# Gate and up projections with their last 64 contraction rows as two 64-row TensorE tiles, weight loads in single pieces, and a prologue with the layer norm per tile

## The chip, the cores and the metric

One NeuronCore of a Trainium2 chip runs the whole program. The metric is device time in microseconds, from the profiler or the device timer; the median of three timed executions of the kernel before is 284.12 us (283.15 to 285.14). The engines are TensorE (PE for its matmuls, PEld for its weight loads), VectorE (DVE), ScalarE (ACT), GpSimd (POOL) and SyncE (SP, which here issues almost all DMAs, in the order of its own queue).

## The reference

The input x has 2048 rows of 448 columns. Four segments of 512 rows are processed in order; there are 16 heads of 28 columns.

```python
h = _layernorm(x) * (1 + ca) + sa
x = x + ga * _A_ref(h, wq, wk, wv, wo, beta)
h = _layernorm(x) * (1 + cb) + sb
x = x + gb * _B_ref(h, w_gate, w_up, w_down)

# A, per segment s and head:
p = softmax(qs @ ks.T * scale + mask)          # causal inside the segment
a_mem = (phi(qs) @ M) / (phi(qs) @ z + 1e-6)   # memory of the segments before
o = sigmoid(beta) * a_mem + (1 - sigmoid(beta)) * (p @ vs)
M = M + phi(ks).T @ vs ;  z = z + sum(phi(ks))
# B:
out = (sigmoid(h @ w_gate) * (h @ w_up)) @ w_down   # 448 -> 1792 -> 448
```

The six vectors sa, ca, ga, sb, cb, gb come from silu(c) @ w_mod. Everything is bf16 with fp32 accumulation.

## The kernel before, in words

The 448 columns are the contraction of every projection. They are cut into three chunks of 128 rows and one of 64 (LW = 64); the weight tiles have four chunks, and rows 64 to 127 of the fourth are zeros, so each projection runs four matmuls of 128 rows. The 1792 columns of gate and up are cut into 14 chunks of 128 (NFC, the index fc).

Per segment: layer norm (class LN: stats, rstd, norm on DVE and POOL, then a transposition into hT, either by DMA on SP's queue in norm_t or by TensorE in pe_chunk, then a scale and shift called modulate); eight projections for q and k and four for v (proj_jobs); per group of four heads hc three groups of logits matmuls (logits, g = 0, 1, 2), each into the one PSUM buffer lg of four banks, emptied by one ACT exponential (line 389); pv, which multiplies by v and by the memory and normalises on DVE; otr, a DMA transposition of the head group's output; wo_tile with the residual and the statistics of the second norm; gate_up for each fc (four gate matmuls into gps, tanh on ACT into tt, four up matmuls into ups, one DVE operation into fT); down, 14 matmuls per 128 rows, and the store.

All other PSUM tiles (gps, ups, acc, mem, pq, pv, dps and so on) come from one ring of four banks (ps_m, tag "m"): a new tile waits for the readers of the one four allocations before it.

The order of the work is written out: there is no scheduler (manual_schedule). The loop at the end goes over the 4 x 4 head groups and their three logits groups; after each it takes jobs from the queue fill until their estimated cost reaches a rate. Operations that would have to wait are put off with later(ns, ...) and come out when the estimated clock has advanced so far. Each engine then works strictly in this order. The loads of the weights are jobs of the queue as well: w_gate, w_up and w_down (load_ffn, load_wd) as one DMA of 128-row chunks each, plus one for the 64-row rest of the first two, all on SP.

A row of gate_up is

```python
for k in range(NK):
    nc.tensor.matmul(gp[:, 0:L], lhsT=wg_sb[:, k, fs], rhs=h[:, k, :], start=(k == 0), stop=(k == NK - 1))
```

and the logits use four 32-row tiles of the array side by side, each with 28 rows of contraction:

```python
nc.tensor.matmul(lg[:, hs, wid:wid + nq], lhsT=kT[r, hc, kb * P:(kb + 1) * P],
                 rhs=qT[r, hc, kb * P:L], start=True, stop=True, tile_position=(HP * hs, 0))
```

The prologue runs 24 warm-up matmuls, the statistics of the first four tiles, one rstd for all four, four norms, copies of wq and wk out of a staging area into padded tiles (pad_copy, wq on ACT, wk on DVE), the columns sa and ca (mod_cols), 16 TensorE transposes, and the first two projections.

## Time and profile before

| quantity | value |
| --- | --- |
| median of three timed executions | 284.12 us (283.15 to 285.14) |
| the profiled execution, its own time | 282.85 us |
| its span, first to last instruction | 281.1 us |
| PE busy | 250.8 us (89%), 2025 matmul records |
| DVE busy | 187.4 us (67%) |
| ACT busy | 140.8 us (50%) |
| POOL busy | 70.8 us (25%) |
| mean granted clock of TensorE | 0.976 |
| HBM read | 10.67 MB |

A matmul is recorded from its start to the end of its pipeline, so busy time of PE overlaps itself; what a matmul costs in a stream is read from the starts of neighbours. In timeline rows consecutive instructions of one line are merged: start, length, engine, line, operation, count, and in brackets the idle time of the engine before the row with what ended it.

### The profile page before, as it was taken

How to read it: one execution, taken by the hardware profiler on the slowest of the kernel's cores; microseconds unless marked ns; L12 is line 12 of the kernel's file. 1: busy time of each engine (PE TensorE's matmuls, PEld its weight loads, DVE VectorE, ACT ScalarE, POOL GpSimd, SP SyncE). 2: the span in 40 equal slices, each digit the busy share in tenths (PEclk: the TensorE clock that was granted, in tenths of full speed). 3: DMA queues.
4: the chain of work that ended last, by engine and by line, in shares of the span. 5: the costliest groups of instructions: out<-in, count | busy, mean ns of one | idle time of the engine just before them, and what ended most of it. 6: DMA issues, size and time to landing. Idle time of an engine off the chain costs nothing. (4 is left out here: it accounts for less than half of the span.)

```text
span 281.1 us, 5201 instructions
## 1 busy us (share of the span) xinstructions
PE 250.8 (89%) x2025; PEld 123.0 (44%) x2048; DVE 187.4 (67%) x426; ACT 140.8 (50%) x171; POOL 70.8 (25%) x127
## 2 busy tenths in 40 slices
PE   1989897983888999998797999889999999899995
PEld 0434453541453544544353554435545444344452
DVE  7578899910679778999655858976577493433321
ACT  2268798583365788765165667562662310133300
POOL 1109434331234034144312213521220040000000
PEclk9999998896699999999999999999999999999999
DMA  5998046699412001301211001141300012100001
GB/s 152 294 249 255 2 105 197 118 198 230 104 21 56 23 19 21 75 21 37 54 54 36 21 0 21 37 57 34 55 19 4 18 37 70 35 0 0 2 16 49
DMA packets 40848, 19.66 MB, mean 70 GB/s; under 512 B 29560, under 2 KB 39928, under 8 KB 40824
## 3 DMA queue, kind: packets, MB, share of 16 engines
q1 hardware_dynamic: 39608, 18.30, 29.2%
q10 hardware_dynamic: 1216, 1.03, 1.3%
q8 instruction: 16, 0.26, 0.4%
q14 instruction: 8, 0.07, 0.1%
HBM read 10.67 MB, written 1.84 MB: 44 GB/s over the span
## 5 line engine op out<-in xcount | busy, mean ns | idle before, releaser
L389 ACT ACTIVATE pT<-lg 128x2048 bf16<-128x2048 f32 (+1 forms) x48 | 76.5, 1594 | 48.6 <-PE lg L386 48.6
L397 POOL TENSOR_SCALAR_AFFINE_SELECT pT<-pT 128x512 bf16<-128x512 bf16 x64 | 43.9, 700 | 87.8 <-ACT pT L389 87.8
L487 DVE SCALAR_TENSOR_TENSOR fT<-tt,ups 128x512 bf16<-128x512 f32 x56 | 37.8, 683 | 35.9 <-PE ups L484 24.6
L479 PE MATMUL gps<-hT,wg_sb 128*128 128x512 bf16 x213 | 57.9, 380 | 3.5 <-DVE hT L257 2.6
L481 ACT ACTIVATE tt<-gps 128x512 f32<-128x512 f32 x56 | 33.0, 596 | 53.9 <-PE gps L479 49.4
L484 PE MATMUL ups<-hT,wu_sb 128*128 128x512 bf16 x219 | 56.6, 379 | 2.4 <-DVE t L439 1.5
L493 PE MATMUL dps<-wd_sb,fT 128*128 128x448 bf16 x224 | 44.2, 353 | 2.3 <-DVE fT L487 2.3
L484 PEld LDWEIGHTS <-wu_sb 128*128 128x128 bf16 x224 | 21.5, 98 | 30.1 <-DVE t L439 2.5
L479 PEld LDWEIGHTS <-wg_sb 128*128 128x128 bf16 x224 | 20.4, 97 | 28.9 <-issue 7.4
L493 PEld LDWEIGHTS <-fT 128*128 128x128 bf16 x224 | 21.4, 98 | 23.5 <-DVE fT L487 2.5
L497 DVE TENSOR_TENSOR ot<-dps,x_sb 128x448 bf16<-128x448 f32 x16 | 9.9, 622 | 23.3 <-PE dps L493 23.3
L411 PEld LDWEIGHTS <-pT 128*128 128x128 bf16 x640 | 18.4, 96 | 4.9 <-issue 2.0
L323 PE MATMUL pv<-wv_sb,hT 128*128 128x448 bf16 x64 | 14.7, 372 | 6.1 <-DVE kT L316 6.1
L238 DVE BATCH_NORM_STATS2 st<-x_sb 128x6 f32<-128x448 bf16 x32 | 19.7, 617 | 0.6
L311 PE MATMUL pq<-hT,wq_sb 128*128 128x512 bf16 x61 | 17.9, 391 | 2.5 <-DVE hT L257 1.3
L242 POOL TENSOR_SCALAR rs<-mv 128x1 f32<-128x1 f32 (+1 forms) x20 | 5.1, 255 | 59.0 <-DVE mv L239 59.0
L411 PE MATMUL acc<-vt,pT 128*128 128x29 bf16 x640 | 18.5, 175 | 1.4 <-ACT vt L325 1.4
L386 PE MATMUL lg<-qT,kT 28*128 28x512 bf16 (+3 forms) x256 | 17.6, 307 | 0.9 <-DVE kT L316 0.8
L311 PE MATMUL pq<-hT,wk_sb 128*128 128x512 bf16 x60 | 17.0, 392 | 1.1 <-ACT qT L314 0.7
L257 DVE TENSOR_SCALAR hT<-hT,cols 128x512 bf16<-128x512 bf16 x24 | 9.6, 447 | 12.4 <-DMA hT<-xn 12.3
L246 DVE TENSOR_SCALAR xn<-x_sb,mv,rs 128x448 bf16<-128x448 bf16 x32 | 15.3, 494 | 2.4 <-POOL rs L243 2.3
L243 POOL TENSOR_TENSOR rs<-rs,mhalf 128x1 f32<-128x1 f32 (+1 forms) x20 | 13.7, 683 | 1.7
(81 smaller groups left out, 232.6 us busy)
## 6 DMA issues: line engine op xcount, KB each, us to landing
wm<-in_w_mod_dram SPq DMA_DIRECT2D x5, 392.0 KB, 4.2
out_dram<-ot SPq DMA_DIRECT2D x16, 112.0 KB, 1.7
wd_sb<-in_B_w_down_dram SPq DMA_DIRECT2D x1, 1568.0 KB
x_sb<-in_A_x_dram SPq DMA_DIRECT2D x3, 448.0 KB, 5.5
wg_sb<-in_B_w_gate_dram SPq DMA_DIRECT2D x1, 1344.0 KB, 11.3
wu_sb<-in_B_w_up_dram SPq DMA_DIRECT2D x1, 1344.0 KB
wm<-in_w_mod_dram ACTq DMA_DIRECT2D x1, 392.0 KB, 6.1
wo_sb<-in_A_wo_dram SPq DMA_DIRECT2D x4, 98.0 KB
```

The costliest lines, as they stand in the source:

```text
L238: nc.vector.bn_stats(st[:], self.srcs[i])
L246: nc.vector.tensor_scalar(self.xn[:, i, 0:D], self.srcs[i], self.mv[:, i, 0:1], self.rs[:, i:i + 1], op0=ALU.subtract, op1=ALU.mult)
L311: nc.tensor.matmul(pq[:, 0:L], lhsT=head_cols(w_sb, k, hc), rhs=h[:, k, :], start=(k == 0), stop=(k == NK - 1))
L386: nc.tensor.matmul(lg[:, hs, wid:wid + nq], lhsT=kT[r, hc, kb * P:(kb + 1) * P], rhs=qT[r, hc, kb * P:L], start=True, stop=True, tile_posi ...
L389: nc.scalar.activation(pT[:, :, w0:w0 + wid], lg[:, :, 0:wid], AF.Exp, scale=scale)
L397: nc.gpsimd.affine_select(out=blk, in_=blk, compare_op=ALU.is_ge, fill=0.0, base=0, pattern=[[0, 4], [1, P]], channel_multiplier=-1)
L411: nc.tensor.matmul(accv[:, qb, hs, 0:ME], lhsT=pT[:, hs, c0:c0 + P], rhs=vt[:, kb, hc * 4 + hs, 0:ME], start=(kb == 0), stop=(kb == qb))
L479: nc.tensor.matmul(gp[:, 0:L], lhsT=wg_sb[:, k, fs], rhs=h[:, k, :], start=(k == 0), stop=(k == NK - 1))
L481: nc.scalar.activation(tt[:], gp[:, 0:L], AF.Tanh, scale=0.5)
L484: nc.tensor.matmul(up[:, 0:L], lhsT=wu_sb[:, k, fs], rhs=h[:, k, :], start=(k == 0), stop=(k == NK - 1))
L487: nc.vector.scalar_tensor_tensor(ft[:], tt[:], 1.0, up[:, 0:L], op0=ALU.add, op1=ALU.mult)
L493: nc.tensor.matmul(dp[:, 0:D], lhsT=fT_of[(s, fc)][:, t * P:(t + 1) * P], rhs=wd_sb[:, fc, :], start=(fc == 0), stop=(fc == NFC - 1))
```

## The change

In gate_up a job now has two column chunks: six gate matmuls (three 128-row chunks for each), then the two 64-row rests of gate and of up as four matmuls on two 64-row tiles of the array (rows 0 to 63 hold the rest of w_gate, rows 64 to 127 that of w_up, in one tile wgu_sb), then six up matmuls. For this the 64 last columns of the normed x are copied once more beside themselves (LN.norm, key "2"), so that both halves of the fourth chunk of hT hold them, and the scale and shift columns likewise (mod_cols).

The loads of w_gate and w_up become three DMAs of one 128-row chunk and one of 64 rows each, that of w_down four DMAs of up to four fc; spread puts one of them behind every second job. The modulate of the second norm is put off with later instead of standing in the job before gate_up. From segment 2 on the wo tiles alternate with left-over gate_up jobs, and the rate is set anew in each segment (pace, KEEP). In the prologue x is loaded ahead of c, the memset that the warm-up reads comes first, rstd runs for two tiles at a time, the warm-up is 20 and later 2 matmuls, the transposes follow each tile's norm, and a third projection stands ahead of the first logits. The normalisation in pv uses inverted coefficients, which saves one small DVE operation.

```diff
-    NWARM, TAIL_GU = 24, 9
+    NWARM, EARLY, KEEP = (20, 2), 2400.0, (0, 2, 2, 4)
-    wg_sb = wts.tile([P, NK, F], BF16)
-    wu_sb = wts.tile([P, NK, F], BF16)
+    wg_sb = wts.tile([P, 3, F], BF16)
+    wu_sb = wts.tile([P, 3, F], BF16)
+    wgu_sb = wts.tile([P, F], BF16)
...
         def norm(self, i):
             nc.vector.tensor_scalar(self.xn[:, i, 0:D], self.srcs[i], self.mv[:, i, 0:1], self.rs[:, i:i + 1],
                                     op0=ALU.subtract, op1=ALU.mult)
+            if self.key[0] == "2":
+                nc.vector.tensor_copy(self.xn[:, i, D:DP], self.xn[:, i, D - LW:D])
...
         later(1500, lambda: ln.norm_t(t), ("ln2", s))
+        if t == TPS - 1:
+            for kc in range(NK):
+                later(6500 + 400 * kc, lambda kc=kc: ln.modulate(kc, 2), ("ln2", s))
...
+        fcs = (f0, f0 + 1)
+        fs = [slice(fc * P, (fc + 1) * P) for fc in fcs]
+        gp = [m_f32("gps") for _ in fcs]
+        for g, f in zip(gp, fs):
+            for k in range(3):
+                nc.tensor.matmul(g[:, 0:L], lhsT=wg_sb[:, k, f], rhs=h[:, k, :], start=(k == 0), stop=False)
+        up = [m_f32("ups") for _ in fcs]
+        tts = []
+        for g, u, f in zip(gp, up, fs):
+            for dst, r, first in ((g, 0, False), (u, LW, True)):
+                nc.tensor.matmul(dst[:, 0:L], lhsT=wgu_sb[r:r + LW, f], rhs=h[r:r + LW, 3, :], start=first,
+                                 stop=not first, tile_position=(r, 0))
+            tt = work.tile([P, L], F32, tag="tt", bufs=3)
+            nc.scalar.activation(tt[:], g[:, 0:L], AF.Tanh, scale=0.5)
+            tts.append(tt)
+        for fc, u, f, tt in zip(fcs, up, fs, tts):
+            for k in range(3):
+                nc.tensor.matmul(u[:, 0:L], lhsT=wu_sb[:, k, f], rhs=h[:, k, :], start=False, stop=(k == 2))
...
+    fill.extend(spread(j0[3:6] + sp(late_consts) + j0[6:10] + [ln1_start(2)] + j0[10:] + ln1_pe_jobs(1) + m[0][0:1]
+                       + j1[:8], early_loads, 2))
+    fill.extend([ln1_start(3)] + m[1][0:1] + j1[8:] + [(1000, prep_b1)])
+    fill.extend(spread(j2[:4] + m[0][1:] + j2[4:8] + [(2000, prep_b2)], [piece_wd(f, min(f + 4, NFC)) for f in range(0, NFC, 4)], 2))
...
+                    for w in wo_jobs(s - 1):
+                        fill.append(w)
+                        if tail and s > 1:
+                            fill.append(tail.pop(0))
+                    fill.extend(tail)
...
+                    pace[0] = (cost(fill) - KEEP[s] * GU) / (12 if s < 3 else 9)
+                debt = run_fill(pace[0] + debt)
```

The first place is TensorE in a gate and up job. Before, for one fc, the last gate matmul and the first up matmul are alike, of 128 rows:

```order
L479 MATMUL gps_1302<-hT_1121,wg_sb_88 128x512
L484 LDWEIGHTS wu_sb_89
L484 MATMUL ups_1309<-hT_1121,wu_sb_89 128x512
```

After the change, with wgu_sb the tile of the two 64-row rests, gps_1391 and gps_1392 the two gate tiles of a job and ups_1399 and ups_1400 its two up tiles:

```order
L509 MATMUL gps_1392<-hT_1144,wg_sb_92 128x512
L514 LDWEIGHTS wgu_sb_94
L514 MATMUL gps_1391<-hT_1144,wgu_sb_94 128x512
L514 LDWEIGHTS wgu_sb_94
L514 MATMUL ups_1399<-hT_1144,wgu_sb_94 128x512
L514 LDWEIGHTS wgu_sb_94
L514 MATMUL gps_1392<-hT_1144,wgu_sb_94 128x512
L514 LDWEIGHTS wgu_sb_94
L514 MATMUL ups_1400<-hT_1144,wgu_sb_94 128x512
L521 LDWEIGHTS wu_sb_93
L521 MATMUL ups_1399<-hT_1144,wu_sb_93 128x512
```

Sixteen matmuls for two fc have become six, four and six, and the four alternate between the two tiles of the array.

The second place is SP's queue around the load of w_down, where segment 2 is projected. Before (hT<-xn_119 are the transpositions of segment 3's first norm, pk those of the memory keys, oT those of attention outputs):

```order
L348 DMA_TRANSPOSE pk<-e 128x4x128 x2
L113 DMA wm_80<-in_w_mod_dram 112x4x448
L253 DMA_TRANSPOSE hT<-xn_119 128x4x128 x2
L348 DMA_TRANSPOSE pk<-e 128x4x128
L606 DMA wd_sb<-in_B_w_down_dram 128x14x448
L253 DMA_TRANSPOSE hT<-xn_119 128x4x128 x2
L452 DMA_TRANSPOSE oT<-ou_121 128x4x128
```

After the change (hT<-xn_122 are the same transpositions):

```order
L374 DMA_TRANSPOSE pk<-e 128x4x128 x2
L117 DMA wm_84<-in_w_mod_dram 112x4x448
L274 DMA_TRANSPOSE hT<-xn_122 128x4x128 x2
L374 DMA_TRANSPOSE pk<-e 128x4x128
L274 DMA_TRANSPOSE hT<-xn_122 128x4x128 x2
L654 DMA wd_sb<-in_B_w_down_dram 128x4x448
L374 DMA_TRANSPOSE pk<-e 128x4x128
L477 DMA_TRANSPOSE oT<-ou_124 128x4x128
L374 DMA_TRANSPOSE pk<-e 128x4x128
L654 DMA wd_sb<-in_B_w_down_dram 128x4x448 x2
L654 DMA wd_sb<-in_B_w_down_dram 128x2x448
```

The last two transpositions of segment 3 have moved ahead of w_down, which comes in four pieces, and w_up's load, which stood ahead of the first of these rows, has moved further up in pieces.

The third place is TensorE at the change from segment 1's last head group to segment 2's first. After the change, two logits groups follow each other (kT_139 is segment 1's, kT_140 segment 2's):

```order
L521 MATMUL ups<-hT,wu_sb 128x512
L412 LDWEIGHTS kT_139
L412 MATMUL lg<-qT_81,kT_139 128x256
L412 LDWEIGHTS kT_140
L412 MATMUL lg<-qT_82,kT_140 128x512
```

Before, a gate and up pair of eight matmuls stood between any two such groups there; now there is none at this place, because a job has become twice as long.

## Rows read from the trace of the kernel before

**Rows 1.** Busy time by stretch, us; x counts instructions; PEclk the granted clock.
```profile
core 0: us, PE busy (x) PEld busy (x) DVE busy (x) ACT busy (x) POOL busy (x), PEclk, DMA share, GB/s
...
47.70:51.00 3.30, 3.08 (x10) 0.83 (x10) 3.27 (x7) 1.33 (x3) 2.03 (x3) 0.50 1.06 352
...
64.80:74.90 10.10, 4.48 (x28) 2.43 (x26) 4.12 (x13) 2.57 (x4) 1.22 (x2) 0.50 1.15 177
...
92.86:134.00 41.14, 39.28 (x382) 19.72 (x386) 35.16 (x82) 28.52 (x35) 12.57 (x19) 1.00 0.14 30
```

**Rows 2.** Waits: engine, line, waited for; us in total, times, longest us.
```profile
DVE hT L257 <- DMA hT<-xn: 12.3, 1, 12.3
...
PE gps L479 <- DVE hT L257: 2.6, 3, 1.3
...
PE dps L493 <- DVE fT L487: 2.3, 3, 1.4
...
PE ups L484 <- DVE t L439: 1.5, 2, 1.2
...
PE pq L311 <- DVE hT L257: 1.3, 2, 0.7
```

**Rows 3.** Timeline of PE around two logits groups among gate and up matmuls.
```profile
99.41 1.03 PE L479 MATMUL gps<-hT,wg_sb 128*128 128x512 bf16 x4
...
102.00 1.03 PE L484 MATMUL ups<-hT,wu_sb 128*128 128x512 bf16 x4
102.96 0.39 PE L386 MATMUL lg<-qT,kT 28*128 28x512 bf16 x4
103.28 1.04 PE L479 MATMUL gps<-hT,wg_sb 128*128 128x512 bf16 x4
...
106.34 0.40 PE L386 MATMUL lg<-qT,kT 28*128 28x384 bf16 x8
106.67 1.04 PE L479 MATMUL gps<-hT,wg_sb 128*128 128x512 bf16 x3
```

**Rows 4.** Timeline of PE, 62 to 72 us.
```profile
62.86 1.16 PE L411 MATMUL acc<-vt,pT 128*128 128x29 bf16 x40 [1.36 <-ACT vt L325]
...
71.18 1.28 PE L323 MATMUL pv<-wv_sb,hT 128*128 128x448 bf16 x3 [5.62 <-DVE kT L316]
```

**Rows 5.** Timeline of DVE, 56 to 70 us.
```profile
56.76 0.69 DVE L316 CAST kT<-pq 128x512 bf16<-128x512 f32 x1
69.79 0.74 DVE L257 TENSOR_SCALAR hT<-hT,cols 128x512 bf16<-128x512 bf16 x2 [12.35 <-DMA hT<-xn]
```

**Rows 6.** Timeline of SP's queue; the length is that of the issue.
```profile
45.64 9.14 SPq L348 DMA_TRANSPOSE pk<-e  x2
...
59.37 0.58 SPq L606 DMA_DIRECT2D wd_sb<-in_B_w_down_dram  x1
60.04 4.58 SPq L253 DMA_TRANSPOSE hT<-xn  x2
```

**Rows 7.** Timeline of the prologue, ACT and PE.
```profile
11.28 1.96 ACT L573 COPY wq_sb<-wd_sb 128x448 bf16<-128x448 bf16 x4 [6.26 <-DMA wd_sb<-in_A_wq_dram]
...
14.59 1.45 ACT L267 ACTIVATE hT<-lntr,cols 128x512 bf16<-128x512 bf16 x2 [1.34 <-PE lntr L265]
...
15.05 1.41 PE L311 MATMUL pq<-hT,wq_sb 128*128 128x512 bf16 x4
```

**Rows 8.** Groups by form: count, busy us, mean ns, idle before.
```profile
L389 ACT ACTIVATE pT<-lg 128x2048 bf16<-128x2048 f32 x32 | 60.1, 1878 | 33.6 <-PE lg L386 33.5
...
L389 ACT ACTIVATE pT<-lg 128x1024 bf16<-128x1024 f32 x16 | 16.4, 1026 | 15.0 <-PE lg L386 15.0
...
L386 PEld LDWEIGHTS <-kT 28*128 28x128 bf16 x256 | 5.2, 92 | 15.0 <-issue 12.3 <-DVE kT L316 1.3
```

**Rows 9.** Timeline of the tail: the last two up matmuls of an fc (PE).
```profile
221.83 0.59 PE L484 MATMUL ups<-hT,wu_sb 128*128 128x512 bf16 x2
```

**Rows 10.** The same place on DVE: the operation that frees that tile.
```profile
222.53 0.69 DVE L487 SCALAR_TENSOR_TENSOR fT<-tt,ups 128x512 bf16<-128x512 f32 x1 [1.04 <-PE ups L484]
```

More of the change, by code (lines that the diff above doesn't have):

```diff
@@ L516, in h2_jobs @@
     def h2_jobs(s):
-        def mods():
-            need(("ln2", s))
-            for kc in range(NK):
-                ln2_of[s].modulate(kc, 2)
-        return [(0, mods)]
+        return [(0, lambda: need(("ln2", s)))]
     def gu_jobs(s):
-        return [(8 * MM, lambda fc=fc: gate_up(s, fc)) for fc in range(NFC)]
+        return [(GU, lambda fc=fc: gate_up(s, fc)) for fc in range(0, NFC, 2)]
     def down_jobs(s):
@@ L581 @@
     ln1_start(1, True)[1]()
[L582 to L583 removed]
     tick(0)
     j0, j1, j2, j3 = [proj_jobs(s) for s in range(NSEG)]
[L586 removed]
+    for c, fn in j0[:3]:
         fn()
@@ L615, in cost @@
         return sum(cst for cst, _ in jobs)
[L617 to L620 removed]
+    pace = [EARLY]
     debt = 0.0
```

140 lines of the change are left out of this document (82 added, 58 removed).

## The prediction

> **What bounds the kernel now.** I read the page's shares first: PE is busy 89% of the span, DVE 67%, ACT 50%. PE has to be taken in order of time, because its share hides stretches of two kinds. In most of the span its matmuls follow each other without a gap: from 99.41 to 102.00 us twelve gate and up matmuls start, 0.216 us each [rows 3]. There, only fewer matmuls help. In the rest, PE waits for something that the order of the work has put behind something slow. The largest place is 62 to 72 us: PE stands still for 1.36 and for 5.62 us, and the second time it waits for a DVE cast [rows 4]. DVE itself has done nothing from 57.45 to 69.79 us, since its next instruction, the modulate of hT, waits 12.35 us for a DMA transposition [rows 5]. That transposition is one of the two that SP issued at 60.04 us, right behind w_down's single load at 59.37; the issue of the two alone took 4.58 us [rows 6]. So the chain is load, transposition, DVE, PE. The clock pays once more: after the pauses it is granted at 0.50 (the 1.2 GHz level) from 64.8 to 74.9 us, with 4.48 us of PE work in it [rows 1].
>
> The smaller waits come from the list of waits: gate matmuls for the modulate (2.6 us in three places), down matmuls for fT (2.3), up matmuls for pv's DVE work (1.5), segment 2's first projection for the modulate (1.3) [rows 2]. After this last one the clock is at 0.50 as well, from 47.7 to 51.0 us, with 3.08 us of PE work [rows 1].
>
> **The change part by part.** All terms are for the profiled execution, 282.85 us with a span of 281.1.
>
> *The 64-row tiles.* Two fc took 16 matmuls, 3.456 us. Now twelve full ones, and four halves that should run as two pairs, fill 14 slots, 3.024 us. The trace has no 64-row tile; the nearest row is the logits, four 32-row tiles of the array. Four up matmuls from 102.00 should end their slots at 102.86, and the logits start at 102.96: 0.10 us to enter. Four logits matmuls of 512 columns then take until 103.28, 0.32 us, where one after the other would need 0.86: they run together, and 0.10 us of it is the way out [rows 3]. So a job pays 0.20 us and gains 0.432, net 0.232; times 28 jobs, **-6.5 us**. Bounds: +5.6 if the halves don't run together (only the 28 x 0.20 us is left), -12.1 if entering and leaving cost nothing. I take the row.
>
> A page of the Trainium skill speaks against a part of this. By the trace, 384 columns and then 128 on the same four tiles, eight matmuls, take 0.33 us from 106.34 to 106.67; the columns alone need 0.21 and the way out 0.10, so the second set's weights were there in time [rows 3]. "TensorE: Matmul & The Clock Gate", section "Part 3: Packing small matmuls", says that weight loads overlap matmuls in flight only when their row groups differ. The second pair of a job uses the row groups of the first; by that rule it would start one weight load later, which is a rival below.
>
> *w_down in four pieces, behind the transpositions.* All four transpositions of segment 3 now stand ahead of it, and w_up's pieces stand singly between earlier transpositions, so that no more than one piece at a time holds the pk transpositions (9.14 us for two at 45.64 us [rows 6]). Gone are 1.36 and 5.62 us of standing [rows 4] and half of 4.48 us at the low clock [rows 1], 9.2 in all; I take **-8.8**, since some wait may stay. What is late next: the output transpositions oT, now behind three pieces. They are needed at the first wo tile, about 12 us of PE work behind the place where those pieces are issued; bound 0 if they come too late.
>
> *Segment 2's first projection.* 1.3 us of wait and half of 3.08 us are at stake, 2.8 in all [rows 1, 2]. But DVE is busy 3.27 of 3.30 us there [rows 1], and the change takes nothing away from it at that place, it only moves the modulate one place forward. I take **-1.2**, between 0 and -2.8.
>
> *The prologue.* wq arrives at 11.28 us and ACT copies it for 1.96 us, until 13.24; its load stands in SP's queue as before. Before, ACT's two parts of hT came at 14.59 to 16.04, behind warm-up, columns and transposes [rows 7]. Now the transposes are done tile by tile before 13.24, so ACT can end at 13.24 + 1.45 = 14.7: **-1.3**. The other bound is a loss: the warm-up now starts about 4 us earlier and ends before the columns' weights are there, so PE pauses. If the clock is then at its lower level, twelve projection matmuls take 0.216 us more each, +2.6.
>
> *The modulate of the second norm put off with later.* The 2.6 us of gate matmuls waiting [rows 2] go, as wo and down jobs lie between: **-2.6**, or 0 if the transposition is late.
>
> *wo tiles between gate_up jobs.* This spreads DVE's bursts, which are behind the waits of down (2.3) and up (1.5) [rows 2]: 3.8, of which I take **-2.8**.
>
> *Coarser jobs.* A job is now 3.2 us, and the loop sometimes leaves nothing between two logits groups. The buffer lg is single: the next group waits for ACT, 1.878 us for a large group and 1.026 for a small one [rows 8]. With about 0.45 us until ACT starts, starts of groups must lie 2.4 or 1.5 us apart. I went through TensorE's new order with 0.216 us for 512 columns, 0.189 for 448, and 0.3 to 0.5 for a group itself: seven places are too short. One small group has nothing behind it (lacking 1.2), four have one short job (0.2 to 0.4 each, 1.4 together), a large one has only pv (0.75), another a v projection and the replication of ga (0.4). Together **+3.7**; before there was at most 0.15. Bounds 0 to 5, since ACT may also be late with a tanh.
>
> *Four banks for one job.* A job takes all four banks of the ring. The fT operation that frees a bank starts 0.27 us after the last up matmul (221.83 + 0.43 = 222.26, to 222.53) and takes 0.69, so it is done 0.96 after it [rows 9, 10]. The second up tile is written again after six gate matmuls, 0.10 and one pair, 1.6 us: 0.65 us to spare, where it was 12 x 0.216 less 0.96, or 1.6. From 92.86 to 134 us DVE is busy 35.16 of 41.14 us [rows 1], and there 0.65 won't always do. Taken **+1.5**; bound: each of the eight jobs behind a pv waits as long as the longest wait of this kind now, 1.2 us [rows 2], +9.6.
>
> Sixteen copies of 64 columns on DVE, the eight small column matmuls and the smaller DVE chain in pv count as nothing: DVE's waits for PE in those places cover them; without that cover the copies would cost under 3 us.
>
> Sum: -6.5 - 8.8 - 1.2 - 1.3 - 2.6 - 2.8 + 3.7 + 1.5 = **-18.0**. From 282.85 this is 264.85. The profiled execution was 1.27 us below the median of the runs, so a median of **266.1 us** is forecast.
>
> **The rivals.**
> - *The wait for DMA moves instead of going.* oT or the transpositions of segment 3 stand behind the pieces all the same. For: transpositions behind a load were held 9.14 and 4.58 us [rows 6]. Against: a piece is at most 448 KB instead of 1568. It gives the 8.8 us back: 274.9. Chance 0.14.
> - *The second pair starts a weight load late.* A load on a row tile takes 0.092 us [rows 8]; 28 of them, 2.6 us: 268.7. Against it is the group of eight above. Chance 0.06. (This is the rule of "TensorE: Matmul & The Clock Gate" cited above.)
> - *The change doesn't do what it says: the halves run one after the other.* Four more slots for two pairs' two, 28 x 0.432 = 12.1: 278.2. Against: rows 3's logits. Chance 0.05.
> - *Slower: the ring of four banks holds PE in every job.* It begins where the second fT operation ends later than 1.6 us after the last up matmul, and it makes the kernel slower when the jobs wait 18.0 / 28 = 0.64 us each on average, that is, when DVE is late by 1.3 us in each. For: DVE's 85% from 92.86 to 134 [rows 1]. Against: over the span DVE is at 67%, and in the tail it waits for PE [rows 10]. At 284.1 and above; chance 0.05.
>
> **How the numbers follow.** The forecast has 0.62, the rest of 0.08 is a time below 258, where the coarser jobs cost nothing and the terms taken in part come whole (-1.6, -1.0, -3.7, -1.5 and -0.4). Its own range is 258 to 270: the good ends just named, and the prologue's 2.6 + 1.3 us the wrong way. The range of 8 in 10 adds the late weights and the moved wait: 258 to 276. Faster by over 1% (below 281.3, which is about what a measurement of this kernel can tell from no change) are all cases but the ring and part of the serial halves with other losses: 0.92. Within 1%: 0.04, slower: 0.04.
>
> **What would show it.** Right: a job's four halves span 0.63 us from the last full gate matmul's slot to the first full up matmul; no DVE wait of over 2 us for hT between 50 and 75 us; the clock at 1.00 from there on; PE standing before a logits group with ACT as the releaser, some 1 us at one place. Wrong: halves that start 0.216 us apart inside a pair; the first wo tile waiting for oT; PE waiting for fT's DVE operation in most jobs; a low clock from 8 to 16 us.

## The result and the profile after

The changed kernel takes 275.02 us (274.24 to 276.8), the kernel before, on the same chip, 284.01 us: ratio 0.969, interval 0.9631 to 0.9749. That is 9.0 us less, where 18.0 were forecast; a second set of timed executions, beside the experiments below, gave 274.84 us and a ratio of 0.9697 (0.9643 to 0.9751). The profiled execution took 276.8 us, the longest of its four, with a span of 275.1 (before: 282.85, below all its timed ones, and 281.1). Where an execution of a kernel below took over 1.5% longer than its fastest (one of 1372 us among them), the median leaves it out.

By the page, PE is busy 246.6 us of it (90%), DVE 185.0 (67%) and ACT 139.2 (51%). Nothing of the balance has changed, so the waits have to be read one by one. PE's own waits, in the manner of [rows 2]:

```profile
PE pv L349 <- DVE kT L342: 4.2, 2, 2.8
PE lg L412 <- ACT pT L415: 3.4, 6, 1.1
PE cp L218 <- DMA wm<-in_w_mod_dram: 2.2, 1, 2.2
PE pwo L486 <- DMA oT<-ou: 2.1, 1, 2.1
PE pq L337 <- DVE hT L296: 1.9, 2, 1.6
...
PE gps L514 <- DVE hT L278: 1.3, 1, 1.3
...
PE pq L337 <- DVE hT L278: 0.9, 2, 0.7
```

Of the waits of [rows 2], dps for fT (2.3 us) is gone and gps for hT is halved. New are lg for ACT, pwo for oT and one of 1.6 us for segment 1's hT at 28 us.

One job (PE, timeline), to be held against [rows 3]:

```profile
168.39 1.47 PE L509 MATMUL gps<-hT,wg_sb 128*128 128x512 bf16 x6
169.79 0.39 PE L514 MATMUL gps<-hT,wgu_sb 64*128 64x512 bf16 x1
169.79 0.39 PE L514 MATMUL ups<-hT,wgu_sb 64*128 64x512 bf16 x1
170.02 0.38 PE L514 MATMUL gps<-hT,wgu_sb 64*128 64x512 bf16 x1
170.02 0.38 PE L514 MATMUL ups<-hT,wgu_sb 64*128 64x512 bf16 x1
170.33 1.47 PE L521 MATMUL ups<-hT,wu_sb 128*128 128x512 bf16 x6
```

The two halves of a pair start within 0.01 us, the second pair 0.23 us behind the first, the first full up matmul 0.31 us behind that: 0.54 us where four slots would take 0.86. From the start of the last full gate matmul to that of the first full up matmul it is 0.85 us in an undisturbed job, a slot of 0.216 and the 0.63 us that were forecast.

The stretch in which the largest gain was looked for. SP's queue first (as [rows 6]), then DVE and PE (as [rows 4, 5]):

```profile
48.39 6.21 SPq L374 DMA_TRANSPOSE pk<-e  x2
...
55.34 2.50 SPq L274 DMA_TRANSPOSE hT<-xn  x2
...
59.20 2.57 SPq L274 DMA_TRANSPOSE hT<-xn  x2
...
66.35 3.07 SPq L654 DMA_DIRECT2D wd_sb<-in_B_w_down_dram  x3
69.52 0.41 SPq L117 DMA_DIRECT2D wm<-in_w_mod_dram  x1
70.03 2.55 SPq L477 DMA_TRANSPOSE oT<-ou  x2
```

```profile
63.13 0.73 DVE L278 TENSOR_SCALAR hT<-hT,cols 128x512 bf16<-128x512 bf16 x2 [5.12 <-DMA hT<-xn]
```

```profile
64.52 1.65 PE L349 MATMUL pv<-wv_sb,hT 128*128 128x448 bf16 x4 [2.81 <-DVE kT L342]
76.51 1.81 PE L486 MATMUL pwo<-wo_sb,oT 128*128 128x448 bf16 x7 [2.13 <-DMA oT<-ou]
```

No part of w_down stands ahead of the last two hT transpositions any more, and still they are issued only at 59.20 us, where it was 60.04, since two key transpositions (pk) hold the queue for 6.21 us. DVE waits 5.12 us where it waited 12.35, PE 2.81 where it waited 5.62. Twelve us later the first wo tile waits 2.13 us for oT, which stands behind three pieces of w_down and one load of wm.

The stretches at the low clock, in the columns of [rows 1]:

```profile
13.18:16.59 3.41, 3.09 (x18) 1.80 (x16) 2.19 (x6) 2.54 (x5) 0.00 (x0) 0.50 1.12 296
30.25:33.66 3.41, 3.14 (x19) 1.29 (x20) 1.74 (x5) 1.11 (x2) 1.59 (x3) 0.50 0.25 64
64.38:67.80 3.42, 3.28 (x53) 1.95 (x53) 1.32 (x8) 0.53 (x1) 0.00 (x0) 0.50 1.16 161
78.03:81.45 3.42, 3.42 (x58) 2.08 (x56) 3.25 (x9) 0.00 (x0) 1.67 (x4) 0.50 0.02 5
```

Four stretches at the 1.2 GHz level, 13.66 us long, where there had been two of 3.41 and 10.24 us: the same length. But PE is busy in 12.93 us of them, before in 3.08 + 4.48 = 7.56: half of it, the cost, has risen from 3.8 to 6.5 us. Each stands at or behind a pause: 2.22 us (cp), 1.58 (hT), 2.81 (kT), 2.13 (oT).

All this is one execution. The profile of the second set, of which the same waits and four such stretches had been expected, has them in part in other places:

```profile
PE pv L349 <- DVE kT L342: 5.3, 2, 3.0
PE pwo L486 <- DMA oT<-ou: 0.8, 1, 0.8
```

The wait for kT in the middle is there again (3.03 us), with the low clock behind it. oT's is 0.82 us and has no low clock behind it, nor has the prologue; in their place the second wait for kT, at 88.6 us, is 2.27 us instead of 1.37, with a low stretch. The three stretches hold 10.00 us of PE work, a cost of 5.0 us. The mean granted clock of the six executions of this set is 0.968 to 0.987, that of the kernel before beside them 0.982 or 0.988.

### The profile page after: what moved, and what is told of

Read it like the earlier page. It is cut to its first block, busy times and chain, and to the rows that moved or that the text cites. A ratio compares the mean times of both kernels' runs of the same rounds, so it can differ in the third digit from the quotient of the medians.

```text
span 275.1 us, 5225 instructions
## 1 busy us (share of the span) xinstructions
PE 246.6 (90%) x2029; PEld 114.7 (42%) x2054; DVE 185.0 (67%) x429; ACT 139.2 (51%) x171; POOL 69.6 (25%) x130
## 4 chain that ended last, share of the span: by engine, by line
PE 44%; DVE 20%; DMA 6%; ACT 3%; issue 3%; SPq 1%; POOL 1%; DVEq 0%; ACTq 0%
PE ups L521 12%; PE dps L530 11%; PE gps L509 10%; PE gps L514 4%; DMA hT<-xn 3%; DVE st L257 3%; PE lg L412 2%; DVE x_sb L489 2%; PE acc L437 2%; DVE fT L524 2%; ACT pT L415 2%; DMA oT<-ou 2%; PE pwo L486 2%; DMA pk<-e 2%; DVE t L470 1%
## 5 line engine op out<-in xcount | busy, mean ns | idle before, releaser
L524 DVE SCALAR_TENSOR_TENSOR fT<-tt,ups 128x512 bf16<-128x512 f32 x56 | 36.8, 684 | 36.7 <-PE ups L521 28.5
L423 POOL TENSOR_SCALAR_AFFINE_SELECT pT<-pT 128x512 bf16<-128x512 bf16 x64 | 41.2, 662 | 67.7 <-ACT pT L415 67.7
L517 ACT ACTIVATE tt<-gps 128x512 f32<-128x512 f32 x56 | 30.3, 595 | 44.9 <-PE gps L514 44.9
L509 PE MATMUL gps<-hT,wg_sb 128*128 128x512 bf16 x155 | 40.4, 380 | 1.0 <-DVE t L465 0.4
L521 PE MATMUL ups<-hT,wu_sb 128*128 128x512 bf16 x164 | 40.2, 381 | 0.5 <-issue 0.5
L521 PEld LDWEIGHTS <-wu_sb 128*128 128x128 bf16 x168 | 14.1, 98 | 25.5 <-issue 12.3
L261 POOL TENSOR_SCALAR rs<-mv 128x1 f32<-128x1 f32 (+2 forms) x21 | 5.2, 248 | 75.9 <-DVE mv L258 75.9
L509 PEld LDWEIGHTS <-wg_sb 128*128 128x128 bf16 x168 | 15.2, 98 | 20.0 <-issue 2.7
L514 PE MATMUL ups<-hT,wgu_sb 64*128 64x512 bf16 x56 | 18.0, 382 | 2.0 <-DVE t L470 1.1
L514 PE MATMUL gps<-hT,wgu_sb 64*128 64x512 bf16 x56 | 17.1, 381 | 1.6 <-DVE hT L278 1.3
L486 PE MATMUL pwo<-wo_sb,oT 128*128 128x448 bf16 x64 | 14.8, 366 | 2.2 <-DMA oT<-ou 2.1
```

The costliest lines, as they stand in the source:

```text
L423: nc.gpsimd.affine_select(out=blk, in_=blk, compare_op=ALU.is_ge, fill=0.0, base=0, pattern=[[0, 4], [1, P]], channel_multiplier=-1)
L509: nc.tensor.matmul(g[:, 0:L], lhsT=wg_sb[:, k, f], rhs=h[:, k, :], start=(k == 0), stop=False)
L514: nc.tensor.matmul(dst[:, 0:L], lhsT=wgu_sb[r:r + LW, f], rhs=h[r:r + LW, 3, :], start=first, stop=not first, tile_position=(r, 0))
L517: nc.scalar.activation(tt[:], g[:, 0:L], AF.Tanh, scale=0.5)
L521: nc.tensor.matmul(u[:, 0:L], lhsT=wu_sb[:, k, f], rhs=h[:, k, :], start=False, stop=(k == 2))
L524: nc.vector.scalar_tensor_tensor(ft[:], tt[:], 1.0, u[:, 0:L], op0=ALU.add, op1=ALU.mult)
```

## The experiments

Times are medians; the changed kernel stands at 274.84 us and the kernel before between 282.97 and 283.31 beside them. Ratios are to the kernel before, with their interval.

**The tiles, taken back.** Halves as plain matmuls:

```diff
-                nc.tensor.matmul(dst[:, 0:L], lhsT=wgu_sb[r:r + LW, f], rhs=h[r:r + LW, 3, :], start=first,
-                                 stop=not first, tile_position=(r, 0))
+                nc.tensor.matmul(dst[:, 0:L], lhsT=wgu_sb[:, f], rhs=h[:, 3, :], start=first,
+                                 stop=not first)
```

> The changed kernel with the four halves of each job as plain matmuls of 128 rows: same number of matmuls, no 64-row tiles. (A half then also adds the 64 rows of the other projection; only the time is looked at.) Theory: the pairs of tiles save two slots of 0.216 us in a job and pay 0.20 us for entering and leaving, net 0.23 us, 28 jobs, 6.5 us. So this kernel takes 274.8 + 6.5 = 281.3 us, and in a job the first full up matmul starts 5 x 0.216 = 1.08 us after the last full gate matmul, where it was 0.85. Rival: PE's time in a job is not what bounds the kernel (the ring of four banks or DVE does), so that the jobs get longer and the waits shorter: then under 3 us, below 278.

Measured: 277.9 us, 0.9821 (0.9765 to 0.9878), 3.1 us more than the changed kernel. PE of this kernel:

```profile
167.63 0.38 PE L514 MATMUL gps<-hT,wgu_sb 128*128 128x512 bf16 x1
167.84 0.38 PE L514 MATMUL ups<-hT,wgu_sb 128*128 128x512 bf16 x1
...
168.49 0.81 PE L521 MATMUL ups<-hT,wu_sb 128*128 128x512 bf16 x3
```

From the first half to the first full up matmul it is 0.86 us, with the tiles 0.54; before the first half stand 0.22 us instead of 0.31. The 0.23 us of a job are there, but only half of their 6.5 us shows in the time. In this kernel PE stands less: its span less PE's busy time is 25.6 us by the page (275.7 and 250.1), that of the changed kernel 28.5 and, in its second profile, 28.2. It has no wait for oT, two stretches of low clock where the changed kernel has four and three, and a mean clock of 0.988 in three of four executions, where the changed kernel has at most 0.987. Part of what the tiles save is handed on to waits that a slower PE does not meet.

**The order of the halves.**

```diff
-        for g, u, f in zip(gp, up, fs):
-            for dst, r, first in ((g, 0, False), (u, LW, True)):
+        for r, first in ((0, False), (LW, True)):
+            for dst, f in zip(up if first else gp, fs):
```

> The changed kernel with the four halves in another order: both gate halves (rows 0 to 63) first, then both up halves (rows 64 to 127), with the tanh of the first chunk after them. Theory: two matmuls run together only if they are neighbours in the order and use different row tiles. Then the second gate half waits for the first, runs beside the first up half, and the second up half follows: three slots where there were two, 0.216 us more in a job, 28 jobs, 6.0 us: 280.8 us, starts 0.22, 0.00, 0.22 us apart. Rival: the array runs ahead far enough to start a half on a free row tile behind one that is held: then the time stays at 274.8 within 1 us.

Measured: 276.29 us, 0.9747 (0.9694 to 0.98): 1.4 us above the changed kernel, with times that overlap (275.23 to 276.95 and 274.33 to 276.78), where three slots would have cost 6.0. The rival's order of starts holds, though not its time to within 1 us; PE of this kernel:

```profile
169.32 0.39 PE L514 MATMUL gps<-hT,wgu_sb 64*128 64x512 bf16 x1
169.33 0.39 PE L514 MATMUL ups<-hT,wgu_sb 64*128 64x512 bf16 x1
169.55 0.38 PE L514 MATMUL gps<-hT,wgu_sb 64*128 64x512 bf16 x1
169.56 0.38 PE L514 MATMUL ups<-hT,wgu_sb 64*128 64x512 bf16 x1
169.87 1.47 PE L522 MATMUL ups<-hT,wu_sb 128*128 128x512 bf16 x6
```

In the program both gps stand first. On the chip an ups has started ahead of the second gps, 0.01 us behind the first: a matmul for a free row tile passes one that waits for an occupied tile.

**The transpositions, in the changed kernel.** Its dM matmuls of segment 0 read the keys' single buffer until 53.4 us. The second key transposition of the row of 6.21 us is segment 1's first; the row ends at 54.60 and one takes 1.22, so this one got away at 53.4, when the buffer was free. The first edit gives segment 1's keys a place of their own, in four tiles of the fT ring, which is idle there; the second issues w_down's pieces with those of w_gate and w_up, one behind each early job; the third kernel has both:

```diff
+        if s == 1:
+            pk[hc] = pipe.tile([P, L], BF16, tag="fT", bufs=NFC + 2, name="pkb")[:].rearrange("p (t q) -> p t q", q=P)
...
-        + [piece(wg_sb, B_w_gate, k) for k in range(NK)] + [piece(wu_sb, B_w_up, k) for k in range(NK)]
+        + [piece(wg_sb, B_w_gate, k) for k in range(NK)] + [piece(wu_sb, B_w_up, k) for k in range(NK)] \
+        + [piece_wd(f, min(f + 4, NFC)) for f in range(0, NFC, 4)]
...
-                       + j1[:8], early_loads, 2))
+                       + j1[:8], early_loads, 1))
```

> The keys of segment 1 go into a buffer of their own instead of the single pk buffer. Theory A (SP's queue stands at the first pk transposition of segment 1 until PE has read segment 0's keys, at 53.4 us, and the hT transpositions of segment 3 stand behind it): these transpositions are issued some 4 us earlier, DVE's wait of 5.1 us at 58 us falls below 1 us, PE's 2.8 us at 62 us and the low clock from 64.4 us go, 3 to 4 us less than the changed kernel (about 271). Theory B (the transpositions are late because DMA is loaded with weights, as the prediction had it): the wait stays above 3 us and the time within 1 us of the changed kernel.

> The pieces of w_down are loaded right behind w_up, one piece behind every job, before segment 2's transpositions, instead of ahead of the oT transpositions. Theory A (oT stood behind three pieces of w_down and one of w_mod): PE's 2.1 us wait for oT at 74 us and the low clock from 78 us go, 2 to 3.5 us less (about 272); DVE's 5.1 us wait at 58 us stays. Theory B (oT is late because its own input is late): PE still waits over 1.5 us before the first wo tile, and the time stays within 1 us. A third outcome: the weights now hold up segment 2's transpositions at 36 us and PE waits longer at 47 us; then nothing is gained.

> Both edits together. Theory A: both waits and both low-clock stretches go, 5 to 7 us less than the changed kernel (268 to 270). If only one of the two is gained, the waits have one cause in common, or the next one behind them (the v projection waiting for a DVE cast at 89 us) takes it up.

Measured: 273.42 us for the buffer alone (0.9631, 0.9577 to 0.9686), 275.89 for the early pieces alone (0.9724, 0.9671 to 0.9777), 270.36 for both (0.9533, 0.9484 to 0.9583). The buffer alone is 1.4 us below the changed kernel, and its slowest execution (273.59) below that one's fastest (274.33); the pieces alone gain nothing; both take 4.5 us off. With the buffer, DVE's longest wait for hT falls from 5.12 to 2.32 us (below 1 was expected), and PE's 2.81 us for kT and the low clock at 64 us are gone, as expected; the gain is less than the 3 to 4 us expected, since the next wait for kT, 2.27 us at 85 us, stays, with a low stretch behind it:

```profile
59.04 0.73 DVE L278 TENSOR_SCALAR hT<-hT,cols 128x512 bf16<-128x512 bf16 x2 [2.32 <-DMA hT<-xn]
```

With the pieces alone, PE no longer waits for oT, as expected, but 2.9 us for kT as before, since the keys still hold the queue.

**The transpositions, in the kernel before.** The same buffer; w_down's whole load right behind w_up's (the first diff); both; and the buffer with w_up and w_down in four pieces each, one behind each of the first eight projections of segment 1 (the second, where steps holds the eight pieces).

```diff
-    fill.extend(ln1_pe_jobs(1) + m[0][0:1] + j1[:8] + [ln1_start(3)] + load_ffn(wu_sb, B_w_up) + m[1][0:1] + j1[8:] + [(1000, prep_b1)])
-    fill.extend(sp(load_wd) + j2[:4] + m[0][1:] + j2[4:8] + [(2000, prep_b2)] + j2[8:] + m[1][1:])
+    fill.extend(ln1_pe_jobs(1) + m[0][0:1] + j1[:8] + [ln1_start(3)] + load_ffn(wu_sb, B_w_up) + sp(load_wd) + m[1][0:1] + j1[8:] + [(1000, prep_b1)])
+    fill.extend(j2[:4] + m[0][1:] + j2[4:8] + [(2000, prep_b2)] + j2[8:] + m[1][1:])
```

```diff
+    for j, st in zip(j1[:8], steps):
+        fill.extend([j, (0, st)])
```

> The kernel before, with one edit: the transposed keys of segment 1 go into four tiles of the fT ring instead of the single buffer pk. Theory: what held SyncE's queue for 9.14 us at 45.64 in the kernel before was not the load of w_up ahead of it but that single buffer, which TensorE still read for segment 0. With a buffer of its own the row falls to 2.5 us, the first two transpositions of segment 3 go out about 6 us earlier, and of the others the third key transposition and w_down's load set the time: VectorE's wait of 12.35 us for hT falls to 7 or 8, TensorE's 5.62 us to about 1.5: 283.2 - 4.5 = 278.7 us. Rival, the reading of the prediction: the load of w_up holds the transpositions and then that of w_down: the row stays over 8 us, 283.2 within 1 us.

> The kernel before with a buffer of its own for segment 1's transposed keys (280.9 us in nine timed executions), looked at for its rows. Theory: SyncE's row of two key transpositions at 45.6 us takes 2.5 us instead of 9.14, and what is left of VectorE's 12.35 us wait for hT (7 to 8 us) now hangs on w_down's load, behind which the last two transpositions of segment 3 stand. Rival: the row still takes over 8 us.

> The kernel before with w_down's load issued right behind w_up's, ahead of the key transpositions, so that it lands while these wait. Theory (two holders, each enough to keep the transpositions late): the last two transpositions of segment 3 are issued at 59.4 instead of 60.0 and land some 4 us earlier, as they do behind no load; TensorE's 5.62 us wait shrinks to about 2: 283.2 - 4 = 279 us. The prediction's reading: w_down's load is what it waits for, and with it away the 7 us of standing and half of the low clock go: 283.2 - 8.8 = 274.4 us.

> The kernel before with both: a buffer of its own for segment 1's transposed keys, and w_down's load right behind w_up's. Theory: both holders are gone, VectorE's wait of 12.35 us for hT falls below 3, TensorE's 1.36 and 5.62 us go and with them the low clock from 64.8 to 74.9 us: the whole 9.2 us that the prediction saw at stake, 274 us. Rival: the next thing is late by then (w_up's load, or the norm's own tiles), and only 4 to 5 us come: 278 to 279 us.

> The kernel before with a buffer of its own for segment 1's transposed keys, and with the loads of w_up and w_down in four pieces each, one behind each of the first eight projections of segment 1. Theory: a transposition issued behind a whole load of 1.6 MB lands 4 to 6 us later than one behind none, whichever load it is, so that with both loads whole the wait only passes from hT to the keys (6.6 us before the memory matmuls when both stood ahead of them). In pieces and with the buffer, nothing is held: no wait of TensorE over 1.5 us from 50 to 75 us, no low clock from 64.6 on, 283.0 - 7.5 = 275.5 us. Rival: the DMA engines themselves are full there, the same bytes keep the transpositions late in pieces as well: 279 to 281 us, with a wait of 3 us or more for a transposition.

Measured: buffer 280.65 us (0.9905, 0.9869 to 0.994); load early 283.34 (1.0011, 0.9973 to 1.0049); both 280.48 (0.993, 0.9893 to 0.9967); buffer and pieces 279.6 (0.9836, 0.9767 to 0.9904). No edit brought more than 3.4 of the 9.2 us, and each fell short of its theory (278.7, 279, 274 and 275.5). Where PE then stood, one line from each of the last four, in this order (the buffer's from its second profile):

```profile
66.81 1.23 PE L413 MATMUL acc<-vt,pT 128*128 128x29 bf16 x40 [5.21 <-DVE kT L316]
```

```profile
58.29 0.57 PE L359 MATMUL dM<-vt,pk 128*128 128x116 bf16 x4 [5.18 <-DMA pk<-e]
```

```profile
58.50 0.57 PE L361 MATMUL dM<-vt,pk 128*128 128x116 bf16 x4 [6.61 <-DMA pk<-e]
```

```profile
56.03 0.57 PE L361 MATMUL dM<-vt,pk 128*128 128x116 bf16 x4 [4.04 <-DMA pk<-e]
```

The wait goes to whichever transposition stands behind the bytes: with w_down's load last it is hT, with the load ahead of the keys it is pk. With the buffer, the row of two key transpositions in SP's queue fell, as its theory said, from 9.14 us to 1.34 and 1.37, but the two hT transpositions behind w_down's load still took 4.39 us to issue, and DVE waited 7.87 us:

```profile
47.16 1.37 SPq L350 DMA_TRANSPOSE pkb<-e  x1
...
56.38 4.39 SPq L253 DMA_TRANSPOSE hT<-xn  x2
```

PE's wait, which this theory put at 1.5 us, is the 5.21 us of the first line above. In the kernel with both edits a key transposition of segment 0, which has no reader to wait for, takes 5.92 us to issue behind the two loads. So the bytes ahead hold a transposition too. Pieces do not change this by themselves. The key transpositions that the kernel with buffer and pieces issues between 44 and 56 us, with the median us to landing:

```profile
pk<-e SPq DMA_TRANSPOSE x3, 6.2
```

The median of the kernel before is 2.5. The 6.2 us are those of one transposition, issued at 45.31 us behind two pieces of w_down, since the landing of the other two is not recorded; the last of the three, issued at 49.99 behind two more pieces, is the one that PE waits for until 56.03. The DMA share fits this, in the columns of [rows 1]; behind it stand the same stretches of the changed kernel with buffer and early pieces (270.36 us), which issues w_up's pieces from 20.3 us on and w_down's from 25.4 to 32.5, where the first kernel does so from 35.2 on and from 44.1 to 49.9:

```profile
34.00:38.00 4.00, 4.00 (x22) 1.54 (x20) 3.79 (x9) 3.87 (x7) 1.90 (x3) 1.00 0.52 141
...
46.00:50.00 4.00, 3.27 (x16) 1.20 (x17) 3.77 (x9) 2.75 (x5) 3.46 (x4) 1.00 1.16 230
50.00:54.00 4.00, 1.50 (x16) 0.83 (x13) 3.88 (x10) 1.71 (x2) 0.63 (x1) 1.00 1.76 299
```

```profile
34.00:38.00 4.00, 3.91 (x44) 1.77 (x41) 3.45 (x11) 2.87 (x3) 1.32 (x3) 0.80 1.09 293
...
46.00:50.00 4.00, 2.44 (x14) 0.97 (x13) 3.74 (x11) 4.00 (x6) 2.40 (x4) 1.00 0.42 89
50.00:54.00 4.00, 4.00 (x34) 2.13 (x33) 3.93 (x10) 3.03 (x4) 1.35 (x2) 1.00 0.96 170
```

The share is over 1 from 38 to 54 us in the one: the DMA engines are busy all this time, and a transposition is late there behind a whole load or a piece. In the other the bytes move earlier, at 34 to 42 us, where the kernel before moved 75 to 101 GB/s, and the keys find the engines half idle at 46 to 50. No run tells whether it is the full engines or the order in the queue that holds a transposition: in the second kernel two for hT, issued from 50.7 us on right behind a load of wm, still land only after 5.6 and 4.7 us, though nothing waits long for them there. In the changed kernel the earlier bytes help only together with the free buffer. (The two kernels differ in more than this stretch; loads that start as early in the kernel before were not tried.)

**DVE's order: wo tiles and modulates.** In the changed kernel, wo tiles never alternating with jobs; alternating in segment 1 too; and the modulates done in the job ahead of gate_up, as before the change:

```diff
-                        if tail and s > 1:
+                        if False:
...
-                        if tail and s > 1:
+                        if tail:
...
-                later(6500 + 400 * kc, lambda kc=kc: ln.modulate(kc, 2), ("ln2", s))
...
-        return [(0, lambda: need(("ln2", s)))]
+        return [(0, mods)]
```

Here mods is need and then the four modulates.

> The changed kernel with the wo tiles never alternating with left-over gate and up jobs: all four of a segment in a burst, in each segment. Theory (the prediction's term): VectorE's bursts then hold up and down matmuls as they did before, 2.8 us more: 277.6 us. Rival: the spread brings nothing, as those waits had other causes: 274.8 within 1 us.

> The changed kernel with the wo tiles of the first segment alternating with left-over gate and up jobs as well, as they do from segment 2 on. Theory: at 77 to 91 us the wo tiles come in one burst, DVE does their residuals and statistics without a pause, and TensorE waits 1.4 to 2.3 us at a pv matmul for the cast of kT that is queued behind them. Spread out, this wait goes: 273 us, no wait of over 1 us for kT at 80 to 90. Rival: the last wo tile then comes later, the norm and its transposition with it, and the first gate matmul of the segment waits for hT by as much: 274.8 or more, with a wait of over 1 us for hT in a gate row at 85 to 92.

> The changed kernel with the four modulates of the second norm in the job ahead of gate_up, as before the change, instead of put off 6.5 us behind the last wo tile. Theory (the prediction's term): the gate matmuls wait for them again, 2.6 us in three places: 277.4 us. Rival: since the wo tiles alternate with gate_up jobs, other work lies between, the time stays at 274.8 within 1 us.

Measured: 280.05 us (0.9888, 0.9824 to 0.9951), 280.12 (0.9894, 0.9842 to 0.9946) and 280.34 (0.9878, 0.984 to 0.9917): each loses 5.2 to 5.5 us, where 2.8 and 2.6 were expected of the first and the last, and the second met its rival. In the burst, gate matmuls wait for the residual's DVE operation, which reads the bank they want:

```profile
129.89 0.81 PE L509 MATMUL gps<-hT,wg_sb 128*128 128x512 bf16 x3 [1.10 <-DVE x_sb L489]
```

In the other two kernels the first gate matmul of segment 0 waits 2 us for the modulate. The clock has fallen shortly before, behind a pv matmul's wait of 1.9 to 2.3 us at 87 us, and with the second pause it stays low for 10.24 us. The kernel with the modulates at once, PE and the window; behind it the window of the changed kernel in its second profile, where the second pause is 1.0 us:

```profile
96.32 1.89 PE L506 MATMUL gps<-hT,wg_sb 128*128 128x512 bf16 x4 [2.00 <-DVE hT L278]
```

```profile
91.60:101.84 10.24, 8.03 (x37) 2.50 (x35) 5.45 (x14) 3.39 (x4) 1.40 (x2) 0.50 0.12 27
```

```profile
88.73:92.14 3.41, 3.41 (x56) 1.99 (x54) 1.68 (x6) 0.53 (x1) 0.39 (x1) 0.50 0.35 79
```

8.03 us of PE work at half speed cost 4.0 us, 3.41 cost 1.7: by these two profiles the second pause costs 2.3 us beyond its own length. It is not this execution alone: the mean clock of the twelve with the modulates at once is 0.956 to 0.975 (the changed kernel's second set: 0.968 to 0.987). What is left of the 5.5 us is not assigned.

**Finer jobs.** A job in two entries of the queue, six gate matmuls and the rest; in the second kernel, left-over jobs go among the wo tiles whole.

> The changed kernel with a gate and up job cut in two entries of the queue (six full gate matmuls, and the rest), so that the loop can put half a job between two logits groups. Theory of the coarser jobs: TensorE waits 3.4 us for the exponential's bank in six places because a whole job is too coarse; by TensorE's order of this kernel the place with nothing between two groups is gone (1.13 us) and two places become 0.58 us short, 2.2 us in all: 273.6 us, and TensorE's wait for ACT before logits groups falls from 3.4 to about 2.2 us. Rival: the waits only change their place, since ACT or DVE are behind there anyway: 274.8 within 0.5 us, with the wait in another line.

> As the kernel with jobs cut in two entries that took 286.5 us, but left-over jobs among the wo tiles go in as whole jobs, so that the wo tiles stand as far apart as in the changed kernel. Theory: the 11.6 us came from the wo tiles, which stood only half a job apart, so that VectorE's residuals and statistics came in a burst and TensorE waited for them (an up half 2.8 us, a memory matmul 2.6 us, and two stretches of low clock): with that taken out the cut gains what was expected of it, 273.6 us. Rival: half a job between two logits groups is itself what costs, since the ring's banks are then held over a logits group: still above 280 us.

Measured: 286.47 us (1.0104, 1.006 to 1.0147) and 277.4 (0.9795, 0.9744 to 0.9845). The first has wo tiles half a job apart, and DVE cannot follow: a memory matmul at 126.55 us waits 1.92 us for the residual's operation. The second has 9.1 of the 11.6 us back, but is still 2.6 us above the changed kernel. Its wait of lg for ACT fell from 3.4 to 2.1 us, as forecast, and another came in its place:

```profile
PE ups L518 <- DVE x_sb L489: 2.2, 2, 1.3
...
PE lg L412 <- ACT pT L415: 2.1, 4, 0.8
```

**On top of the best.** To the kernel of 270.36 us, the k casts of segment 3's last two head groups on ACT and the four modulates 100 ns apart; then 30 warm-up matmuls as well.

```diff
-                later(6500 + 400 * kc, lambda kc=kc: ln.modulate(kc, 2), ("ln2", s))
+                later(6500 + 100 * kc, lambda kc=kc: ln.modulate(kc, 2), ("ln2", s))
...
-            jobs.append((4 * MM, lambda hc=hc: proj_qk(s, hc, wk_sb, kT_of[s], "dve")))
+            jobs.append((4 * MM, lambda hc=hc: proj_qk(s, hc, wk_sb, kT_of[s], "act" if s == 3 and hc > 1 else "dve")))
...
-    NWARM, EARLY, KEEP = (20, 2), 2400.0, (0, 2, 2, 4)
+    NWARM, EARLY, KEEP = (30, 2), 2400.0, (0, 2, 2, 4)
```

> The changed kernel with own buffers for segment 1's transposed keys and w_down's pieces among the early loads (270.4 us together), and two edits more: the k casts of segment 3's last two head groups on ScalarE, and the modulates of the second norm 100 ns instead of 400 ns apart, so that the fourth stands ahead of pv's VectorE work. Theory: TensorE's wait of 2.26 us for the cast of kT at 81 us and the 1.01 us for hT's fourth chunk at 89 go, and with the first the low clock after it (3.41 us long, 1.6 us lost): 270.4 - 2.3 - 1.0 - 1.6 = 265.5 us. Rival: VectorE stays the one that is late there, with hT's transposition 2 to 3 us after the last norm as the next wait: 268 to 270 us, with a wait of over 1.5 us for hT in the first gate matmul.

> The kernel with the two edits more, and 30 instead of 20 warm-up matmuls at the start. Theory: TensorE then works until 9.8 us instead of 7.6, when the weights of the columns have landed, the clock is not lowered from 11.7 to 18.5 us, where the first projections ran at half speed (1.98 and 1.91 us instead of 1.0 each): 2.2 us less than the same kernel with 20. Rival: the fall of the clock does not hang on that pause but on the thin work from 9.8 to 14 us (columns and transposes): the first projections stay at half speed in this run, and the time is the same within 0.5 us or, where the warm-up ends later than the landing, longer.

Measured: 269.51 us (0.9526, 0.948 to 0.9572) and 270.27 (0.9536, 0.9475 to 0.9596), where 265.5 and 2.2 less were expected. In the first, the wait of 2.26 us for kT at 81 us and the low clock behind it went, and PE's idle time hardly changed: 0.98 us at the first gate job, for DVE's pv, and 0.81 at an acc, for POOL, came instead. In the profile with 30 warm-ups the clock does not fall before 29.8 us (span 266.5, clock 0.991), as its theory had it, but the median is not better. The first of the two stays the fastest kernel of this study, by a margin on the 270.36 us that the intervals do not confirm.

## Why the prediction was right in direction and wrong in size

The direction held, and 275.0 us lies within the range of 8 in 10 (258 to 276), but not within the forecast's own (258 to 270), and the gain is half of the forecast, 9.0 us against 18.0. Of the prediction's own signs, the job's halves and PE's 1.13 us before a logits group came as named; DVE's wait for hT stayed above 2 us (5.12), and of the signs of being wrong there came the first wo tile's wait for oT and, in one of two profiles, a low clock in the prologue.

A sum over TensorE shows where the gain is missing. By the pages, the span less PE's busy time is 30.3 us before (281.1 and 250.8), 28.5 after (275.1 and 246.6) and 28.2 in the second profile (273.9 and 245.7). The low clock cost 3.8 us before, 6.5 and 5.0 after. With 28 x 0.23 = 6.4 us for the tiles, the first profile should be 6.4 + 1.8 - 2.7 = 5.5 us shorter, the second 6.4 + 2.1 - 1.2 = 7.3; the spans are 6.0 and 7.2 us shorter. (The medians differ by more, since the profiled executions of the two kernels lie on opposite sides of theirs.) So the tiles' own time came as forecast, and all terms on waits and clock, -11.5 together, came to between +0.9 and -0.9.

By the prediction's steps:

- **The tiles, -6.5.** Right in each step: 0.10 in, two slots, 0.10 out, 0.23 us in a job, and no late second pair. Taken back, they were worth 3.1 us, as the experiment showed: a faster PE arrives earlier at what is late anyway, which no term had reckoned with. The rule of the Trainium skill, "TensorE: Matmul & The Clock Gate", "Part 3: Packing small matmuls", that weight loads overlap matmuls in flight only when row groups differ, is not borne out: the second pair follows after 0.23 us, one slot of 0.216 and no load of 0.092.
- **w_down behind the transpositions, -8.8. The step that failed.** It read the 9.14 us issue of [rows 6] as the effect of w_up's load and took it that, with pieces and another order, nothing would hold the transpositions. Two shorter windows split this row of the kernel before; PE's dM row, below them, says what it waited for:

```profile
45.64 1.35 SPq L348 DMA_TRANSPOSE pk<-e  x1
53.59 1.19 SPq L348 DMA_TRANSPOSE pk<-e  x1
52.36 1.19 PE L359 MATMUL dM<-vt,pk 128*128 128x116 bf16 x16
```

  The first transposition went out in 1.35 us, right behind w_up's load. The second, segment 1's first, was issued when the reads of the single key buffer ended, at 53.55 us. So the buffer made the row long, as the runs with a second one confirm (1.34 and 1.37 us), and the change left it as it was: the last two hT transpositions are issued at 59.20 us instead of 60.04. Behind it lay a second holder, the bytes ahead in the queue: another order of the same bytes gives the wait to another transposition. Of 1.36 + 5.62 us of standing and 2.2 us for the clock, 9.2 in all, the first profile has 2.81 + 2.13 and half of 3.28 + 3.42, 8.3 in all; the second has 3.03 + 0.82 and half of 3.42, 5.6 in all, and 2.6 us more at the next wait for kT (2.27 us instead of 1.37, and half of 3.41). (The 1.36 us have ACT as their releaser in [rows 4]; that they hang on the transposition was not shown.) The prediction had named oT as the next that could be late and given it no term; it waited 2.13 and 0.82 us. The rival "the wait for DMA moves instead of going" gave 274.9. Of it oT's wait behind the pieces came, but hT stood behind the keys and not behind a piece; that its time agrees to 0.1 us is luck, since other terms were off as well.
- **Segment 2's first projection, -1.2.** The waits of 1.3 us are 0.9, and the low clock of 47.7 to 51.0 us is gone. But a fall of the clock now stands at 30.25, behind a pause of 1.58 us for segment 1's hT, which no step had foreseen; it costs half of 3.14 us.
- **The prologue, -1.3.** Right where the clock held. The first logits start at 18.34 us in the first profile, with one projection of 0.86 us more done than before (18.11): 0.6 us gained, though the clock is low from 13.18 to 16.59. In the second, where it does not fall there, they start at 17.84: 1.1 us. The copy of wq starts at 12.34 us, not at 11.28 as taken. The pause ahead of the columns that the other bound named is there, 2.22 and 1.52 us, and so, in one profile of two, is the low clock.
- **The modulate, -2.6, and the wo tiles, -2.8.** Right in sign, and undone they cost more, 5.5 and 5.2 us, the first in good part through the low clock that its pause prolongs. Each was undone alone, in a kernel where the other waits stand as they do, and the two need not add up.
- **Coarser jobs, +3.7.** Right: 3.4 us in six places, the longest 1.13 us where nothing stands between two groups. The expectation that finer jobs would give it back was not met.
- **Four banks, +1.5.** Too small. By the starts of the halves, seven of the 28 jobs lose 0.1 to 1.2 us beyond the 0.85 that a job needs from its last gate to its first full up matmul, 4.3 us together. One of them:

```profile
131.59 0.37 PE L514 MATMUL ups<-hT,wgu_sb 64*128 64x512 bf16 x1 [0.41 <-ACT tt L517]
```

  In the kernel with the tiles taken back the same seven jobs lose 2.1 us beyond the 1.08 that such a job needs. So 2.2 of the 6.5 us of the tiles go to these waits.

The sizes that were read from a row of the same kind (a job with tiles, coarser jobs) came within 0.3 us. Those that rested on a cause put behind a merged row of a queue, or on a wait simply going, did not. How the missing 9 us divide among the waits stays open, since a pause and the clock that follows it cannot be told apart by undoing one edit, and two profiles of one kernel have them in different places.

## What to carry to other kernels

Before a wait for a transfer is booked as a gain, ask of each instruction in that queue whether a buffer holds it and what bytes stand ahead of it: in this kernel a new order of the same bytes handed the wait on, and the gain came from earlier bytes together with a free buffer. A merged issue row of a queue hides which of its instructions waited; a shorter window shows each one, and then the reader of its buffer can be looked for. Terms for a faster engine and for its waits do not simply add up: a faster one meets waits that a slower one does not. And a pause is priced with its clock: here a second one of 2 us within a stretch of low clock cost 2.3 us beyond itself, one of 1 us behind it nothing. Before rows of one execution are booked, a second profile of the same kernel shows which of them recur.

## What the runs showed of the hardware

- Halves on the two row tiles start 0.003 to 0.004 us apart, and in the kernel with both gate halves first an up half passes a gate half that waits for its own row tile: the four still take two slots (1.942 us from a job's last full gate matmul to its last full up matmul, against 1.939).
- The weight load of the second pair costs nothing visible, though its row tile is in use.
- Key transpositions landed 2.5 us after their issue in the median before; one issued where the DMA share was over 1, behind two pieces of 448 KB, landed after 6.2 us.
- In the first profile of the changed kernel, pauses of 1.58, 2.13, 2.22 and 2.81 us each had 3.41 us of clock 0.50 at or behind them, pauses of 1.13, 1.34 and 1.37 us none. The length of one pause does not tell it: in the kernel before the clock fell at 47.65 us behind two pauses of 0.66 and 0.68 us, and with the wo tiles alternating in segment 1 too, a pause of 3.06 us that ended at 64.2 us had no low clock. With a pause of 2.00 us inside a low stretch it lasted 10.24 us.
